# Set attention into a top-1 mixture of experts: every expert on every token, or tokens sorted on chip by expert

## The chip, the cores and the metric

The program runs on one NeuronCore of a Trainium2 chip. The metric is the device time of one execution in microseconds (us). The kernel before takes 8194.92 us, the median of three runs (8193.73 to 8201.59).

The engines are named as in the profile: PE is TensorE (PEld is its weight load), DVE is VectorE, ACT is ScalarE, POOL is GpSimd, SP is SyncE. Each works through its own list of instructions in order and waits on semaphores for the others.

## What is computed

The reference, shortened. Two steps, with B = 4 batches of N = 11456 tokens of C = 128 channels, 45824 tokens in all.

```python
def mab(q, kv):                                  # in the reference's _attn_ref
    s = scale * (q @ kv.transpose(0, 2, 1))
    s = s - s.max(-1, keepdims=True)
    a = np.exp(s); a /= a.sum(-1, keepdims=True) + 1e-09
    return a @ kv
h = mab(I, x)                                    # 32 inducing points attend to all tokens of the batch
x = mab(x, h)                                    # every token attends to the 32 rows of h

logits = x @ w_gate + modality_bias[modality_id] # 8 experts
e_idx = np.argmax(logits, axis=1)
gate_w = softmax(logits)[e_idx]
for e in range(8):                               # only the tokens whose top expert is e
    h = np.maximum(x[mask] @ w1[e], 0.0)         # 128 -> 1024
    out[mask] = gate_w[mask, None] * (h @ w2[e]) # 1024 -> 128
```

## The kernel before

All loops are unrolled; a scheduler sets the order of each engine's instructions, and the buffers of the pools (four PSUM buffers tagged pt, two for oep) set how far the engines may run ahead.

Stage one (lines 77 to 125) computes h batch by batch, 128 tokens at a time: 90 tiles of a batch, the last with 64 tokens. A tile is loaded (L90), transposed on PE in float32 (L92), copied (L94), multiplied with the inducing points (L96), and passed through a running maximum and sum (L98 to L119), in which every tile waits for the one before it.

Stage two (lines 127 to 205) takes the same 360 tiles again. Each is loaded (L135), goes through its attention (L137 to L162) and its gate (L165 to L187), and then through all eight experts: for an expert eight matmuls with 128x128 weights of w1 (L197), eight ReLUs that bring them from PSUM to SBUF as bfloat16 (L198), eight matmuls with w2 (L200), and two DVE operations that scale the result with the token's gate weight, which is zero for the seven experts that the token did not choose, and add it up (L202, L203). All DMAs go through POOL's queue: the tokens, the modality ids (L169), the weights (L65, L69) and the output (L205).

## Time and profile before

| | |
|---|---|
| median of three runs | 8194.92 us |
| the profiled execution, first to last instruction | 8197.6 us |
| PE busy | 6172.4 us, 75% |
| ACT busy | 4934.1 us, 60% |
| DVE busy | 3673.2 us, 45% |
| POOL busy | 789.4 us, 10% |
| instructions | 158845 |

The profiled execution's own time is its span; it lies 2.7 us above the median. Busy time is the time in which at least one instruction of the engine ran. Matmuls are pipelined, so that the mean duration of one is much longer than the distance from one to the next: what counts on PE is the distance. The rows come further down.

### The profile page before, as it was taken

The page shows a single profiled execution, that of the slowest core. Times are in us where ns is not written, and L with a number is a line of the kernel's source. Part 1 is how long each engine was busy: PE and PEld are TensorE (multiplying, and loading weights), DVE is VectorE, ACT ScalarE, POOL GpSimd, SP SyncE. Part 2 cuts the span into 40 slices and gives each one's busy share as a digit, 9 for nine tenths or more (in the row PEclk, how much of TensorE's full clock was granted, in tenths as well). Part 3 has the DMA queues.
Part 4 walks back from the last instruction along what each step waited for, and adds up shares of the span by engine and source line. Part 5 has one row for each costly group of instructions (what it writes and reads, how often), then busy time and mean ns, then how long its engine had stood idle before and what let it go on. Part 6 is the DMA issues. An engine that isn't in the chain of part 4 may idle for free.

```text
span 8197.6 us, 158845 instructions
## 1 busy us (share of the span) xinstructions
PE 6172.4 (75%) x51124; PEld 4334.1 (53%) x51124; DVE 3673.2 (45%) x16227; ACT 4934.1 (60%) x26281; POOL 789.4 (10%) x1452
## 2 busy tenths in 40 slices
PE   3444444488888888888888888888888888888888
PEld 1111111266666666666666666666666666666665
DVE  3444444444444444444444444444444444444444
ACT  1222222267776776767776767767766677677766
POOL 2111111100000000000000000000000000000000
PEclk9999999987888887888888878888888788888888
DMA  1000000000000000000000000000000000000000
GB/s 55 15 15 15 15 15 15 14 9 8 9 9 9 9 9 8 9 9 9 9 9 9 9 8 9 9 9 9 9 9 9 8 9 9 9 9 8 9 9 6
DMA packets 49176, 89.41 MB, mean 11 GB/s; under 512 B 29008, under 2 KB 29008, under 8 KB 48336
## 3 DMA queue, kind: packets, MB, share of 16 engines
q0 software_dynamic: 48336, 79.26, 3.4%
q8 instruction: 399, 6.54, 0.3%
q14 instruction: 441, 3.61, 0.2%
HBM read 55.71 MB, written 23.46 MB: 10 GB/s over the span
## 4 chain that ended last, share of the span: by engine, by line
PE 63%; ACT 13%; DVE 12%; issue 11%; POOL 1%; DMA 0%; ACTq 0%; POOLq 0%
PE hp L197 28%; PE oep L200 18%; ACT hid L198 6%; PE sp L96 3%; PE op L117 3%; PE xmp L160 3%; PE lp L165 2%; PE xtTp L92 2%; PE sp L141 2%; ACT pexp L108 2%; ACT ex L150 2%; PE pT L113 1%; PE aTp L156 1%; DVE xtT L94 1%; ACT alpha L105 1%
## 5 line engine op out<-in xcount | busy, mean ns | idle before, releaser
L198 ACT ACTIVATE hid<-hp 128x128 bf16<-128x128 f32 x23040 | 4305.5, 297 | 1466.8 <-PE hp L197 1277.2
L197 PE MATMUL hp<-xmb,w1sb 128*128 128x128 bf16 x23040 | 3992.6, 244 | 174.6 <-ACT hid L198 6.6
L200 PE MATMUL oep<-w2sb,hid 128*128 128x128 bf16 x23040 | 3402.3, 245 | 2.8 <-ACT hid L198 2.8
L197 PEld LDWEIGHTS <-w1sb 128*128 128x128 bf16 x23040 | 2319.1, 113 | 639.8 <-issue 403.5
L200 PEld LDWEIGHTS <-hid 128*128 128x128 bf16 x23040 | 2124.6, 106 | 658.8 <-ACT hid L198 77.5
L202 DVE TENSOR_SCALAR scaled<-oep,gm 128x128 f32<-128x128 f32 x2880 | 1010.4, 351 | 2231.8 <-PE oep L200 2231.8
L203 DVE TENSOR_TENSOR oacc<-oacc,scaled 128x128 f32<-128x128 f32 x2880 | 840.5, 292 | 98.9
L98 ACT ACTIVATE ssb<-sp 32x128 f32<-32x128 f32 x360 | 95.5, 265 | 1025.4 <-PE sp L96 1025.4
L135 POOL DMA_DIRECT2D xt<-in_x_dram x360 | 192.9, 536 | 4283.5 <-PE oep L200 4198.0
L113 PE MATMUL pT<-ident,pexp 32*128 32x32 f32 x360 | 111.3, 309 | 624.3 <-ACT pexp L108 624.3
L156 PE MATMUL aTp<-ident,a_sb 128*32 128x128 f32 x360 | 115.2, 320 | 605.7 <-DVE a_sb L154 605.7
L113 PEld LDWEIGHTS pT<-ident,pexp 32*128 32x128 f32 x360 | 63.5, 176 | 786.6 <-ACT pexp L108 786.6
L156 PEld LDWEIGHTS aTp<-ident,a_sb 128*32 128x32 f32 x360 | 34.8, 97 | 645.5 <-DVE a_sb L154 645.5
L169 POOL DMA_DIRECT2D mid<-in_moe_modality_id_dram x360 | 200.2, 556 | 1506.4 <-DVE midf L171 1451.5
L160 PE MATMUL xmp<-aT,h_sb 32*128 32x128 f32 x720 | 240.6, 427 | 133.6 <-DVE aT L158 133.6
L96 PE MATMUL sp<-xtT,indT 128*32 128x128 f32 x720 | 228.1, 420 | 141.4 <-DVE xtT L94 137.5
L90 POOL DMA_DIRECT2D xt<-in_x_dram x360 | 192.9, 536 | 1368.4 <-PE op L117 1333.3
L165 PE MATMUL lp<-wg,xm 128*128 128x8 f32 x720 | 208.9, 364 | 137.9 <-DVE xm L162 137.9
L117 PE MATMUL op<-xt,pTsb 128*32 128x128 f32 x720 | 228.5, 421 | 102.1 <-DVE pTsb L115 102.1
L165 PEld LDWEIGHTS lp<-wg,xm 128*128 128x128 f32 x720 | 175.0, 302 | 229.0 <-DVE xm L162 229.0
L143 ACT ACTIVATE ssb<-sp 128x32 f32<-128x32 f32 x360 | 70.9, 197 | 326.5 <-PE sp L141 326.5
L100 DVE TENSOR_REDUCE mnew<-ssb 32x1 f32<-32x128 f32 x360 | 98.4, 273 | 367.1 <-ACT ssb L98 367.1
(69 smaller groups left out, 3767.2 us busy)
## 6 DMA issues: line engine op xcount, KB each, us to landing
xt<-in_x_dram POOLq DMA_DIRECT2D x712, 64.0 KB, 2.1
out_dram<-oacc POOLq DMA_DIRECT2D x356, 64.0 KB, 1.8
mid<-in_moe_modality_id_dram POOLq DMA_DIRECT2D x356, 1.0 KB, 2.0
w1f<-in_moe_w_dram POOLq DMA_DIRECT2D x1, 4096.0 KB, 15.8
w2f<-in_moe_w_dram POOLq DMA_DIRECT2D x1, 4096.0 KB, 29.3
xt<-in_x_dram POOLq DMA_DIRECT2D x8, 32.0 KB, 2.0
out_dram<-oacc POOLq DMA_DIRECT2D x4, 32.0 KB, 1.8
mid<-in_moe_modality_id_dram POOLq DMA_DIRECT2D x4, 0.5 KB, 1.8
```

What stands on the lines that cost most here:

```text
L96: nc.tensor.matmul(sp[:, :r], indT, xtT[:, :r], start=True, stop=True)
L113: nc.tensor.transpose(pT[:r], pexp[:, :r], ident[:m, :m])
L117: nc.tensor.matmul(op, pTsb[:r], xt[:r], start=True, stop=True)
L156: nc.tensor.transpose(aTp[:, :r], a_sb[:r], ident[:r, :r])
L160: nc.tensor.matmul(xmp[:, :r], hb, aT[:, :r], start=True, stop=True)
L165: nc.tensor.matmul(lp[:r], xm[:, :r], wg, start=True, stop=True)
L169: nc.gpsimd.dma_start(out=mid32[:r], in_=mid_all[b * N + r0: b * N + r0 + r, :])
L197: nc.tensor.matmul(hp[:, :r], w1sb[:, e, f * 128:(f + 1) * 128], xmb[:, :r], start=True, stop=True)
L198: nc.scalar.activation(hid[:, f, :r], hp[:, :r], AF.Relu)
L200: nc.tensor.matmul(oep[:r, :], hid[:, f, :r], w2sb[:, e, f, :], start=(f == 0), stop=(f == nF - 1))
L202: nc.vector.tensor_scalar_mul(scaled[:r], oep[:r], gm[:r, e:e + 1])
L203: nc.vector.tensor_add(oacc[:r], oacc[:r], scaled[:r])
```

## The change

The stages are rebuilt batch by batch as three phases, which the program writes in the order A(0), B(0), A(1), B(1), C(0), A(2), B(2), C(1), A(3), B(3), C(2), C(3).

- Phase A (h) takes 16 tiles at once, a chunk; a batch has five chunks of 16 tiles and one of 10. One DMA on SP's queue loads 1 MB. Sixteen transposes on PE go through four DVE copies of 512 columns; four score matmuls of 512 columns and 32 rows follow, each in its own 32 columns of the array (tile_position), then one maximum, one exponential, four transposes, one copy and sixteen small matmuls with the tokens. Each chunk keeps its own maximum; the chunks are put together at the batch's end.
- Phase B computes h@W1 for all experts once (32 rows by 1024 columns for each), goes through the chunks a second time (the transposed tokens of phase A are still in SBUF), finds logits, top expert and gate weight for the whole batch, and computes for every token a slot such that the tokens of one expert stand together, padded to tiles of 256. A row of 72 bytes per token (32 attention weights as bfloat16, already multiplied with the gate weight, and the token's number) is written to that slot in DRAM: 90 indirect DMAs from POOL, 128 rows each. One DMA on SP brings the sorted list back.
- Phase C goes through the 52 sorted tiles. PE and DVE each read the tile's expert number into a register. DVE copies that expert's part of h@W1 to stg; eight matmuls with K = 32 and 256 columns give the hidden layer, four ReLUs of 512 columns (two on ACT, two on DVE) bring it to SBUF, sixteen matmuls with w2 at a register address give 256 rows of output, ACT copies them, and two indirect DMAs from POOL write the rows to their tokens.
- The weights are loaded by ACT's queue; w2 goes through the two buffers tagged xn, which the tokens use too, and is cast on POOL.

The core of the diff (`phase_b`'s gate arithmetic on whole-batch tiles and the end of phase A are cut):

```diff
...
+P = 128
+T = 256
+CH = 16
+OOB = 1 << 20
...
+    NT = (N + E * (T - 1)) // T
+    NS = NT * T // P
...
-    sb = ctx.enter_context(tc.tile_pool(name="sb", bufs=4))
-    ps = ctx.enter_context(tc.tile_pool(name="ps", bufs=4, space=bass.MemoryType.PSUM))
-    ps_big = ctx.enter_context(tc.tile_pool(name="ps_big", bufs=2, space=bass.MemoryType.PSUM))
+    xpool = ctx.enter_context(tc.tile_pool(name="xpool", bufs=2))
+    xtpool = ctx.enter_context(tc.tile_pool(name="xtpool", bufs=NCH))
+    sb = ctx.enter_context(tc.tile_pool(name="sb", bufs=2))
+    sm = ctx.enter_context(tc.tile_pool(name="sm", bufs=2))
+    bat = ctx.enter_context(tc.tile_pool(name="bat", bufs=1))
+    bat2 = ctx.enter_context(tc.tile_pool(name="bat2", bufs=2))
+    hidp = ctx.enter_context(tc.tile_pool(name="hidp", bufs=2))
+    ps_h = ctx.enter_context(tc.tile_pool(name="ps_h", bufs=2, space=bass.MemoryType.PSUM))
+    ps_o = ctx.enter_context(tc.tile_pool(name="ps_o", bufs=1, space=bass.MemoryType.PSUM))
+    ps = ctx.enter_context(tc.tile_pool(name="ps", bufs=3, space=bass.MemoryType.PSUM))
...
-    w1sb = singles.tile([D, E, F], BF)
...
+    fill = bat2.tile([P, NS, RW], I32, tag="srt")
+    nc.gpsimd.memset(fill, 0)
+    nc.gpsimd.memset(fill[:, :, m // 2:m // 2 + 1], OOB)
...
-            xt = sb.tile([P, D], F32)
-            nc.gpsimd.dma_start(out=xt[:r], in_=x[b, r0:r0 + r, :])
-            xtTp = ps.tile([D, P], F32, tag="pt")
-            nc.tensor.transpose(xtTp[:, :r], xt[:r], ident[:r, :r])
-            xtT = sb.tile([D, P], F32)
...
+        nc.scalar.dma_start(out=d.rearrange("(p s) w -> p s w", p=P), in_=fill)
...
+    def load_weights():
+        nc.scalar.dma_start(out=w1f, in_=moe_w1.rearrange("e d f -> d e f"))
+        for e in range(E):
+            w2f = xpool.tile([P, nF, D], F32, tag="xn")
+            nc.scalar.dma_start(out=w2f, in_=moe_w2[e].rearrange("(o p) d -> p o d", p=P))
+            nc.gpsimd.tensor_copy(w2sb[:, e], w2f)
...
+            nc.tensor.matmul(s[32 * g:32 * g + 32, 0:k, :], lhsT, xT.rearrange("d (i g) n -> d i g n", g=G)[:, 0:k, g, :],
+                             start=True, stop=True, tile_position=(0, 32 * g))
...
+            xn = xpool.tile([P, CH, D + 4], F32, tag="xn")
+            nc.sync.dma_start(out=xn[:, 0:nj, 0:D], in_=x[b, 0:J * P, :].rearrange("(p j) d -> p j d", j=J)[:, c * CH:c * CH + nj, :])
...
+            nc.gpsimd.memset(xn[:, :, D:D + 1], 1.0)
...
+                    nc.tensor.transpose(tp[:, k, 0:w], xn[0:w, G * i + k, 0:D], ident[:w, :w])
...
+                nc.vector.tensor_copy(xT[:, G * i:G * i + full, :], tp[:, 0:full, :])
...
+            s = scores(indT, xT, c)
...
+            nc.vector.reduce_max(mxall[:, c:c + 1], s[:, 0:nb, :], axis=AX.XY)
...
+            nc.scalar.activation(p[:, 0:nb, :], s[:, 0:nb, :], AF.Exp, bias=nbias, scale=scale)
...
+                nc.tensor.transpose(pTp[:, i, :], p[:, i, :], ident)
...
+            nc.scalar.copy(pT[:, 0:nb * G, :].rearrange("p c m -> p (c m)"), pTp[:, 0:nb, :].rearrange("p i c -> p (i c)"))
...
+                    nc.tensor.matmul(o[32 * g:32 * g + 32, :], pT[0:w, k, :], xn[0:w, k, 0:D + 1],
+                                     start=(i == mine[0]), stop=(i == mine[-1]), tile_position=(0, 32 * g))
...
+                    nc.tensor.matmul(hp[32 * g:32 * g + 32, e, :], hT, w1f[:, 2 * e2 + e, (F // G) * g:(F // G) * (g + 1)],
+                                     start=True, stop=True, tile_position=(0, 32 * g))
+            nc.scalar.copy(hw[:, 2 * e2:2 * e2 + 2, :], hp)
...
+            s = scores(hT, xTs[c], c)
...
+            nc.scalar.activation(s2[:, 0:nb, :], s[:, 0:nb, :], AF.Copy, scale=scale)
...
+                nc.tensor.transpose(tt[:, i, :], s2[:, i, :], ident)
...
+            nc.vector.reduce_max(mx[:, 0:nt], ttv, axis=AX.X)
...
+            nc.vector.tensor_tensor(exc, ttv, mx[:, 0:nt].unsqueeze(2).to_broadcast([P, nt, m]), op=OP.subtract)
+            nc.scalar.activation(exc, exc, AF.Exp)
...
+                nc.tensor.transpose(et[:, i, :], exc[:, G * i:G * i + G, :].rearrange("p g m -> p (g m)"), ident)
...
+            nc.vector.tensor_copy(eT[:, 0:full, :], et[:, 0:full, :])
...
+                nc.tensor.matmul(up[:, i, :], eT[:, i, :], bd.rearrange("p g e -> p (g e)"), start=True, stop=True)
...
+        pay = bat.tile([P, NJ, RW], I32, tag="pay")
+        nc.vector.tensor_tensor(pay.bitcast(BF)[:, :, 0:m], ex, gs.unsqueeze(2).to_broadcast([P, NJ, m]), op=OP.mult)
+        nc.gpsimd.memset(pay[:, :, m // 2 + 1:RW], 0)
+        nc.vector.tensor_scalar(pay[:, :, m // 2], tok, b * N, None, op0=OP.add)
...
+        nc.vector.tensor_tensor_scan(cum.rearrange("p e j -> p (e j)"), ones[:, 0:1].to_broadcast([P, E * NJ]), oh.rearrange("p e j -> p (e j)"), 0.0, op0=OP.mult, op1=OP.add)
...
+        row = bat2.tile([P, NJ], I32, tag="row")
+        nc.vector.scalar_tensor_tensor(row, pi[:, 0, :], float(NS), pi[:, 1, :], op0=OP.mult, op1=OP.add)
...
+        nc.vector.tensor_scalar(eidi, eid, float(E - 1), None, op0=OP.min)
...
+        for j in range(NJ):
+            w = width(j)
+            i = nc.gpsimd.indirect_dma_start(
+                out=srt_d[b][:, :], out_offset=bass.IndirectOffsetOnAxis(ap=row[0:w, j:j + 1], axis=0),
+                in_=pay[0:w, j, :], in_offset=None)
...
+        srt = bat2.tile([P, NS, RW], I32, tag="srt")
+        nc.sync.dma_start(out=srt, in_=srt_d[b].rearrange("(p s) w -> p s w", p=P))
...
+        for t in range(NT):
+            if t % 2 == 0:
+                k = min(4, NS - 2 * t)
+                etp = ps.tile([P, 4, P], BF, tag="ps")
+                rep = sb.tile([P, 4, G, m], BF, tag="rep")
+                nc.vector.tensor_copy(rep[:, 0:k], srt.bitcast(BF)[:, 2 * t:2 * t + k, 0:m].unsqueeze(2).to_broadcast([P, k, G, m]))
+                for q in range(k):
+                    nc.tensor.transpose(etp[:, q, :], rep[:, q].rearrange("p g m -> p (g m)"), identb)
+                eT4 = sb.tile([P, 4, P], BF, tag="eT4")
+                nc.vector.tensor_copy(eT4[:, 0:k, :], etp[:, 0:k, :])
+            eT = eT4[:, (t % 2) * 2:(t % 2) * 2 + 2, :]
+            ev = nc.values_load(eidi[0:1, t:t + 1], engines=(PE, DVE), min_val=0, max_val=E - 1,
+                                skip_runtime_bounds_check_because="clamped on the chip")
+            stg = sb.tile([P, 2, P], BF, tag="stg")
+            nc.vector.tensor_copy(stg, hw[:, ds(ev, 1), :].rearrange("p o (r f) -> p (o r) f", r=2))
+            hp = [ps_h.tile([P, 2, T], F32, tag=f"hp{q}", bufs=1, name=f"hp{q}") for q in range(4)]
+            for r in range(2):
+                for g in range(G):
+                    nc.tensor.matmul(hp[g][:, r, :], stg[32 * g:32 * g + 32, r, :], eT[32 * g:32 * g + 32, :, :],
+                                     start=True, stop=True, tile_position=(32 * g, 0))
+            hid = hidp.tile([P, G, 2, T], BF, tag="hid")
+            for g in range(G):
+                if g % 2 == 0:
+                    nc.scalar.activation(hid[:, g], hp[g], AF.Relu)
+                else:
+                    nc.vector.tensor_scalar_max(hid[:, g], hp[g], 0.0)
+            op = ps_o.tile([P, 2, D], F32, tag="op")
+            for s in range(2):
+                for f in range(nF):
+                    nc.tensor.matmul(op[:, s, :], hid[:, f // 2, f % 2, s * P:(s + 1) * P], w2sb[:, ds(ev, 1), f, :].rearrange("p o d -> p (o d)"),
+                                     start=(f == 0), stop=(f == nF - 1))
+            ob = sb.tile([P, 2, D], F32, tag="ob", bufs=3)
+            nc.scalar.copy(ob, op)
+            for s in range(2):
+                i = nc.gpsimd.indirect_dma_start(
...
+                    in_=ob[:, s, :], in_offset=None, bounds_check=B * N - 1, oob_is_err=False)
...
-            xmb = sb.tile([D, P], BF)
...
-            for e in range(E):
-                for f in range(nF):
-                    hp = ps.tile([P, P], F32, tag="pt")
-                    nc.tensor.matmul(hp[:, :r], w1sb[:, e, f * 128:(f + 1) * 128], xmb[:, :r], start=True, stop=True)
-                    nc.scalar.activation(hid[:, f, :r], hp[:, :r], AF.Relu)
-                for f in range(nF):
-                    nc.tensor.matmul(oep[:r, :], hid[:, f, :r], w2sb[:, e, f, :], start=(f == 0), stop=(f == nF - 1))
-                scaled = sb.tile([P, D], F32)
-                nc.vector.tensor_scalar_mul(scaled[:r], oep[:r], gm[:r, e:e + 1])
-                nc.vector.tensor_add(oacc[:r], oacc[:r], scaled[:r])
...
+    load_weights()
+    phase_a(0)
+    phase_b(0)
+    for b in range(B):
+        if b + 1 < B:
+            phase_a(b + 1)
+            phase_b(b + 1)
+        phase_c(b)
```

How the instructions stand now, at the three places on which the prediction's terms rest.

PE at the start, the first tiles of stage one before (xt is the token tile, pexp its exponentials):

```order
L92 MATMUL xtTp<-ident,xt 128x128
L96 MATMUL sp<-xtT,indT 32x128
L113 MATMUL pT<-ident,pexp 128x32
L117 MATMUL op<-xt,pTsb 32x128
L92 MATMUL xtTp<-ident,xt 128x128
```

And now, the end of chunk 0 and chunk 1 of A(0) (xn holds 16 token tiles):

```order
L214 MATMUL o_t<-xn,pT 32x129 x16
L190 MATMUL tp<-ident,xn 128x128 x16
L155 MATMUL s<-xT,indT 32x512 x4
L204 MATMUL pTp<-ident,p 128x128 x4
L214 MATMUL o_t<-xn,pT 32x129 x16
```

The same four steps stand in the same order; one round now serves 16 tiles, and nothing of the next chunk stands between the steps of one.

PE in the experts, before (the first tile of stage two):

```order
L160 MATMUL xmp<-aT,h_sb 128x128
L165 MATMUL lp<-wg,xm 128x8
L197 LDWEIGHTS w1sb
L197 MATMUL hp<-xmb,w1sb 128x128
L197 LDWEIGHTS w1sb
```

And now, between two tiles of C(0) (eidi holds the tiles' expert numbers, L427 is the matmul with w2, L416 that of the hidden layer):

```order
L427 LDWEIGHTS hid
L427 ISA
L427 MATMUL op<-w2sb,hid 128x128
L409 TENSOR_LOAD eidi
L416 LDWEIGHTS stg
L416 MATMUL hp_1959<-eT_1900,stg 128x256
```

Every matmul with w2 has an ISA instruction before it that works out its address from the register; TENSOR_LOAD fills the register once per tile; the hidden matmuls of a later tile stand among the w2 matmuls of an earlier one.

POOL before, from the end of stage one into stage two:

```order
L90 DMA xt<-in_x_dram 128x128 x89
L90 DMA xt<-in_x_dram 64x128
L135 DMA xt<-in_x_dram 128x128 x5
L169 DMA mid_15413<-in_moe_modality_id_dram 128x2
L135 DMA xt<-in_x_dram 128x128
```

And now, from the end of B(0) into C(0) (L382 is the scatter of the sorted rows, L432 that of the output):

```order
L382 DMA srt_136<-pay,row 13312x18 x90
L181 MEMSET xn 128x16 x2
L327 MEMSET pay 128x90
L181 MEMSET xn 128x16 x4
L254 MEMSET bd 128x36
L336 AFFINE_SELECT oh<-oh 128x8
L342 MEMSET prev 128x1
L432 DMA out_dram<-ob,srt 45824x128 x2
L382 DMA srt_138<-pay,row 13312x18 x90
L432 DMA out_dram<-ob,srt 45824x128 x6
```

A(1)'s memsets for its chunks 2 and 3 now stand behind the 90 scatters of batch 0, and all but two of C(0)'s output scatters behind the 90 of batch 1.

## Rows read from the trace of the kernel before

**Rows 1.** The page's line of PE's, ACT's and the other engines' busy time.

```profile
PE 6172.4 (75%) x51124; PEld 4334.1 (53%) x51124; DVE 3673.2 (45%) x16227; ACT 4934.1 (60%) x26281; POOL 789.4 (10%) x1452
```

**Rows 2.** Stretches: length, busy time by engine (count), PEclk, DMA share, GB/s.

```profile
0.00:40.00 40.00, 0.44 (x1) 0.18 (x1) 10.06 (x13) 1.28 (x1) 19.53 (x20) 1.00 0.74 217
40.00:1622.00 1582.00, 715.06 (x2164) 260.44 (x2164) 670.70 (x3633) 339.42 (x1440) 197.15 (x369) 1.00 0.05 15
1622.00:8194.00 6572.00, 5456.95 (x48959) 4073.53 (x48959) 2992.42 (x12584) 4593.38 (x24840) 572.75 (x1064) 0.81 0.03 9
```

**Rows 3.** The page's chain of work that ended last, by engine and line.

```profile
PE 63%; ACT 13%; DVE 12%; issue 11%; POOL 1%; DMA 0%; ACTq 0%; POOLq 0%
PE hp L197 28%; PE oep L200 18%; ACT hid L198 6%; PE sp L96 3%; PE op L117 3%; PE xmp L160 3%; PE lp L165 2%; PE xtTp L92 2%; PE sp L141 2%; ACT pexp L108 2%; ACT ex L150 2%; PE pT L113 1%; PE aTp L156 1%; DVE xtT L94 1%; ACT alpha L105 1%
```

**Rows 4.** Timeline in stage two: start, us, engine, line, operation, tiles.

```profile
3000.35 0.35 DVE L202 TENSOR_SCALAR scaled<-oep,gm 128x128 f32<-128x128 f32 x1 [0.89 <-PE oep L200]
...
3000.97 0.43 PEld L200 LDWEIGHTS <-hid 128*128 128x128 bf16 x5
3001.02 0.52 PE L200 MATMUL oep<-w2sb,hid 128*128 128x128 bf16 x5
...
3001.92 0.35 DVE L202 TENSOR_SCALAR scaled<-oep,gm 128x128 f32<-128x128 f32 x1 [0.89 <-PE oep L200]
```

**Rows 5.** Groups by line and shape: busy us, mean ns | idle before.

```profile
L198 ACT ACTIVATE hid<-hp 128x128 bf16<-128x128 f32 x22784 | 4263.1, 298 | 1424.9 <-PE hp L197 1238.2
...
L94 DVE COPY xtT<-xtTp 128x128 f32<-128x128 f32 x356 | 103.8, 291 | 46.9 <-PE xtTp L92 0.6
...
L137 PE MATMUL xtTp<-ident,xt 128*128 128x128 f32 x356 | 100.2, 281 | 0.0
...
L189 DVE CAST xmb<-xm 128x128 bf16<-128x128 f32 x356 | 80.6, 226 | 12.0
...
L150 ACT ACTIVATION_READ_ACCUMULATOR ex<-ssb,nmx 128x1 f32 x356 | 66.3, 186 | 0.0
...
L198 ACT ACTIVATE hid<-hp 128x64 bf16<-128x64 f32 x256 | 42.4, 226 | 41.9 <-PE hp L197 38.9 <-PE oep L200 2.7
...
L94 DVE COPY xtT<-xtTp 128x64 f32<-128x64 f32 x4 | 0.9, 225 | 0.1
```

**Rows 6.** Timeline in stage one, two tiles in succession.

```profile
44.68 0.28 DVE L118 TENSOR_TENSOR O<-O,op 32x128 f32<-32x128 f32 x1 [0.61 <-PE op L117]
...
45.43 0.64 PE L96 MATMUL sp<-xtT,indT 128*32 128x128 f32 x2 [0.38 <-DVE xtT L94]
...
49.07 0.28 DVE L118 TENSOR_TENSOR O<-O,op 32x128 f32<-32x128 f32 x1 [0.73 <-PE op L117]
```

**Rows 7.** Groups of POOL: building the descriptors of one DMA.

```profile
L169 POOL DMA_DIRECT2D mid<-in_moe_modality_id_dram x360 | 200.2, 556 | 1506.4 <-DVE midf L171 1451.5 <-DVE oacc L203 34.8 <-DMA mid<-in_moe_modality_id_dram 10.2
...
L69 POOL DMA_DIRECT2D w2f<-in_moe_w_dram x1 | 2.8, 2761 | 0.0
L51 POOL DMA_DIRECT2D indT<-in_inducing_dram x1 | 1.8, 1840 | 0.4 <-issue 0.4
```

**Rows 8.** Timeline at the start: a DVE cast and a POOL DMA beside it.

```profile
20.91 4.43 DVE L67 CAST w1sb<-w1f 128x8192 bf16<-128x8192 f32 x1 [10.05 <-DMA w1f<-in_moe_w_dram]
21.16 4.29 POOL L169 DMA_DIRECT2D mid<-in_moe_modality_id_dram  x1 [9.20 <-DMA w1f<-in_moe_w_dram]
```

**Rows 9.** DMA issues: count, KB each, median us from issue to landing.

```profile
mid<-in_moe_modality_id_dram POOLq DMA_DIRECT2D x356, 1.0 KB, 2.0
w1f<-in_moe_w_dram POOLq DMA_DIRECT2D x1, 4096.0 KB, 15.8
w2f<-in_moe_w_dram POOLq DMA_DIRECT2D x1, 4096.0 KB, 29.3
```

More of the change, by code (lines that the diff above doesn't have):

```diff
@@ new lines @@
+    identb = singles.tile([P, P], BF)
+    nc.vector.tensor_copy(identb, ident)
+    ones = singles.tile([P, P], F32)
+    nc.vector.memset(ones, 1.0)
+    tri = singles.tile([P, P], F32)
+    nc.gpsimd.affine_select(out=tri, in_=ones, compare_op=OP.is_gt, fill=0.0, base=0,
+                            pattern=[[1, P]], channel_multiplier=-1)
+    selm = singles.tile([P, m], F32)
+    nc.vector.reduce_sum(selm, ident.rearrange("p (g m) -> p m g", g=G), axis=AX.X)
+    sel = singles.tile([P, G, m], F32)
@@ new lines @@
+    for g in range(G):
+        nc.vector.tensor_copy(sel[:, g, :], selm)
+    one1 = singles.tile([1, 1], F32)
+    nc.vector.memset(one1, 1.0)
+    indT = singles.tile([D, m], F32)
+    ind_sb = sm.tile([m, D], F32, tag="ind_sb")
+    nc.sync.dma_start(out=ind_sb, in_=inducing)
+    indTp = ps.tile([D, m], F32, tag="ps")
+    nc.tensor.transpose(indTp, ind_sb, ident[:m, :m])
+    nc.vector.tensor_copy(indT, indTp)
+    wg = singles.tile([D, E], F32)
+    nc.sync.dma_start(out=wg, in_=moe_w_gate)
@@ new lines, in chunk_tiles, with blocks, width, scores @@
+    def chunk_tiles(c):
+        return list(range(c * CH, min((c + 1) * CH, NJ)))
+    def blocks(c):
+        t = chunk_tiles(c)
+        return (len(t) + G - 1) // G
+    def width(j):
+        return P if j < J else R
+    def scores(lhsT, xT, c):
+        nb = blocks(c)
+        s = ps.tile([P, 4, P], F32, tag="ps")
+        for g in range(G):
+            full = [i for i in range(nb) if c * CH + G * i + g < J]
+            k = len(full)
+            nc.tensor.matmul(s[32 * g:32 * g + 32, 0:k, :], lhsT, xT.rearrange("d (i g) n -> d i g n", g=G)[:, 0:k, g, :],
+                             start=True, stop=True, tile_position=(0, 32 * g))
+            for i in range(k, nb):
+                j = c * CH + G * i + g
+                w = width(j) if j < NJ else 0
+                lo = 0
+                if w:
+                    nc.tensor.matmul(s[32 * g:32 * g + 32, i, 0:w], lhsT, xT[:, G * i + g, 0:w], start=True, stop=True, tile_position=(0, 32 * g))
+                nc.tensor.matmul(s[32 * g:32 * g + 32, i, w:P], lhsT, xT[:, g, w:P], start=True, stop=True, tile_position=(0, 32 * g))
+        return s
@@ new lines, with phase_c @@
+    out2 = out
+    def phase_c(b):
+        st = state[b]
+        hw, srt, eidi = st["hw"], st["srt"], st["eidi"]
+        eT4 = None
+        for t in range(NT):
[15 more added lines that the diff above has]
+            for r in range(2):
+                for g in range(G):
+                    nc.tensor.matmul(hp[g][:, r, :], stg[32 * g:32 * g + 32, r, :], eT[32 * g:32 * g + 32, :, :],
+                                     start=True, stop=True, tile_position=(32 * g, 0))
+            hid = hidp.tile([P, G, 2, T], BF, tag="hid")
+            for g in range(G):
+                if g % 2 == 0:
[11 more added lines that the diff above has]
+                i = nc.gpsimd.indirect_dma_start(
+                    out=out2[:, :], out_offset=bass.IndirectOffsetOnAxis(ap=srt[:, 2 * t + s, m // 2:m // 2 + 1], axis=0),
+                    in_=ob[:, s, :], in_offset=None, bounds_check=B * N - 1, oob_is_err=False)
+                tc.declare_no_dep(i.ins, group="out", reason="tokens are unique")
+                tc.add_to_no_dep_group("out", i.ins)
```

342 lines of the change are left out of this document (216 added, 126 removed).

## The prediction, made before the changed kernel was timed

> **What bounds the kernel now.** I read four views in this order. The busy line [rows 1] shows no engine above 75%, so an average tells little, and the stretches [rows 2] split the span: 40 us of start, 1582 us of stage one, 6572 us of stage two, 80% of the 8197.6 us. Stage two has 360 tiles, so 18.3 us each. The chain [rows 3] puts PE first, with the expert matmuls L197 and L200 alone at 46% of the span. The timeline [rows 4] shows the beat: from the scaling of one expert to that of the next are 3001.92 - 3000.35 = 1.57 us, in which PE does 16 matmuls, 98 ns each; five in a row without a wait load weights in 0.43 us, 86 ns each. So stage two is 360 x 8 experts x 1.57 us = 4520 us of experts, and the remaining 2050 us, 5.7 us a tile, is the chain of small steps between two tiles. Stage one is a chain too: 4.39 us from one tile's L118 to the next [rows 6], 360 times, while its PE is busy 45% of the stretch [rows 2].
>
> **What the change takes away.** Seven of eight experts: 360 x 128 = 46080 expert matmuls become 4 x 52 tiles x (8 + 16) = 4992. And the chains: 16 tiles go through one round instead of one. The forecast is therefore not a difference but a new sum, built from durations in these rows. It has three unknown prices that no row shows: m, the time of a sorted tile of 256 tokens in phase C; d, POOL's time for one indirect DMA; and AB, the time of phases A and B of a batch.
>
> **m.** PE: 16 matmuls with w2 at 98 ns [rows 4], 1.57 us. Each has an ISA instruction that works out an address: below, nothing (it hides under the weight load before it); above, 186 ns, the shortest row of an instruction that only moves engine state (the accumulator read) [rows 5], 3.0 us in all. I take 0.1 us, half of that row, since it too goes through the sequencer one by one: 1.6 us. Eight hidden matmuls of 256 columns in four row groups: 8 x 0.17 (twice the 86 ns) = 1.4 us one after another, a quarter of it if the four run at once; I take 0.8. Two transposes 0.2. One TENSOR_LOAD: between nothing, since it stands several rows before its use, and 2.0 us, the landing of a 1 KB DMA [rows 9]; I take 0.4, because PE is one stream but the array still holds work. Sum 4.6, and I use m = 4.5. Beside it ACT has two ReLUs of 512 columns, by the slope of the L198 rows [rows 5] 0.298 + 384 x 0.072/64 = 0.73 us, and one copy of 256, 0.44: 1.9 us. DVE has two of 512 at 0.291 + 384 x 0.066/64 = 0.69 us, a staging copy of 256 (0.3 from the 226 ns cast), and every second tile one repeat and one PSUM copy (0.5 + 0.69): 2.3 us. Both lie beside PE. The ends for m are 2.5 (DVE, with a hand-over of the single op buffer) and 1.57 + 3.0 + 1.4 + 0.2 + 2.0 = 8.1.
>
> **d.** A plain DMA of 128 rows costs POOL 0.56 us; one of 4096 single elements 1.84 us, one of 8192 pieces 2.76 us [rows 7]. An indirect one has 128 rows but must read an index for each, so it lies between: I take 1.2, bounds 0.54 and 2.76. Landing is 2.0 us [rows 9], but eight may be under way, so the landing doesn't limit it. S = 90 d = 108 us is the scatter of a batch.
>
> **AB.** Phase A, a chunk of 16 tiles: 16 transposes at 0.2 us (between the 86 ns beat and 281 ns alone [rows 5]), then the last copy of 0.69: 4.0 us. Four score matmuls of 512 columns in float32: a pair for 128 columns takes 0.64 us [rows 6]; with two thirds of it, 0.43, growing with the columns (an estimate: the rest is the way through the array), 512 take 1.7 us; 6.8 one after another, 1.7 at once; I take 3.0, nearer the lower end because each holds its own 32 columns of the array. Maximum and bias 1.0, exponential 0.8, four transposes 0.9, ACT's copy 0.7, sixteen small matmuls 4.0 (0.43 each if serial, and four in a row share one column group). That is 14.4 us, 5.6 chunks: 81 us. Phase B's chunk, by the same prices: scores 3.0, copy 0.7, transposes 0.9, maximum and subtraction 1.4, exponential 0.7, transposes 0.9, copy 0.7, the last matmuls 1.2, waits 0.4: 9.9 us, 55 us in all. The end of A (a dozen tiny steps) 9, h@W1 10, the gate of the whole batch 18 (13 operations of 720 columns at 0.8 us, one of 2880, twenty small ones at 0.15). AB = 173 us; all prices at their ends give 130 and 215.
>
> The Trainium skill, page "TensorE: Matmul & The Clock Gate", section "Part 3: Packing small matmuls — row/col tiling", says that matmuls in different column groups run at once and gives 2.38 times for three. By it the four score matmuls would take an estimated 2.9 us. No row here shows it, since the kernel before has no such matmul; if they ran one after another the sum would rise by (6.8 - 3.0) x 5.6 x 2 x 4 = 170 us.
>
> **How the parts lie in time.** POOL's order decides (the third listing in the change). The scatter of batch 0 starts when B(0) ends, and A(1) can go on for about two and a half chunks (35 us): then its small matmuls need the memset that stands behind the 90 scatters. So S is paid nearly in full there. At the end of B(1) the same: all but two of C(0)'s output DMAs are queued behind S; with three ob buffers, four tiles fit in before PE must wait. So C is S + 48 m. A(2) starts on PE after C(0), and so on.
> Start: w1 is 4 MB in 15.8 us [rows 9], ACT waits for it before the fills of the sorted lists (4 x 0.96 MB, at w1's rate 14 us), then eight w2 loads go two by two through the buffers that the first token chunks need: 55 us until phase A can start (ends 45 and 75), against 40 before.
> Sum: 55 + AB 173 + S 108 + (AB - 35) 138 + three times (S 108 + 48 x 4.5 = 216 and, twice, AB 173) + 52 x 4.5 = 234 + 5. That is 55 + 173 + 108 + 138 + 324 + 648 + 346 + 234 + 5 = 2031 us. In short T = 717 + 360 d + 196 m. The profiled span and the median of the runs before differ by 0.03%, so nothing is added for that.
>
> One row speaks against putting 776 DMAs on POOL: while DVE's cast of w1 ran 4.43 us, a 128-row DMA beside it took POOL 4.29 us instead of 0.56 [rows 8]. If DVE's two SBUF copies of a tile (about 0.55 us) hold POOL up that way, a tile costs POOL 2.4 + 0.55 = 2.95 us, still under m, and nothing is added; where POOL is the bound (below) 196 x 0.55 = 108 us are.
> The Trainium skill, page "SBUF — State Buffer", section "Who interferes with whom", states the rule: a DVE operation in a two-port mode and GpSimd exclude each other for the whole instruction. The trace agrees, with those 4.29 us.
>
> **The rivals.**
> 1. Register work bounds phase C. For it: nothing in the trace shows an address from a register, and it stands 16 times in each tile. Against it: the weight load before it gives it 86 ns of cover. At the upper end, m = 8.1: 717 + 432 + 1588 = 2737 us; from m = 6 on I count it here (2325).
> 2. POOL bounds. At d = 2.76 two output DMAs are 5.5 us, more than m: 717 + 994 + 196 x 5.5 = 2789 us, with DVE in the way 2900. Against it: 128 rows are far fewer pieces than 8192.
> 3. Everything runs as smoothly as plain work: m = 2.5, d = 0.54: 717 + 194 + 490 = 1401 us. For it: the scheduler mixes two tiles on PE, so waits are filled. Against it: it needs all three prices at the low end.
> 4. Slower than before: POOL builds an indirect DMA row by row, each row a small job of its own. All 776 stand in one queue, so T = 717 + 776 d, and it passes 8195 at d = 9.6 us, 75 ns a row. The dearest POOL row is 2.76 us [rows 7], a third of that.
> 5. The sort gains less than its count: 52 tiles for 44.75 of tokens is built in, 16% of phase C, and inside the sum already; there is no way back to eight experts.
>
> **How the numbers follow.** Forecast 2031 us (m from 3.2 to 6, d from 0.8 to 2: 1630 to 2610), chance 0.47. Rival 1 0.20, rival 2 0.12, rival 3 0.18, rival 4 0.02, others 0.01. The range runs from 1500, which takes in the upper half of rival 3, to 2700, which takes in most of rival 1 and leaves out most of rival 2. A difference of 0.2%, 16 us, is about what a measurement of this kernel can tell from none; only rival 4 ends on the other side. Faster 0.97, same 0.01, slower 0.02.
>
> **What would show it.** In phase C: the distance between two ob copies, 4.5 us, with PE the bound; ISA or issue time between w2 matmuls would be rival 1, ob copies waiting for POOL's DMAs rival 2. The scatter L382: 90 DMAs in 108 us, three gaps of about 90 us in which PE and ACT stand still before C, and one in A(1). First token transposes at 55 us. A chunk of A every 14 us, of B every 10. Wrong would be a phase C in which DVE or ACT is the bound, scatters that hide under other work, or a first chunk at 40 us or before.

## The result, and the profile after

The changed kernel takes **1900.42 us** (1898.82 to 1900.96, four runs) against 8197.38 us before (8193.73 to 8201.59): a ratio of **0.2318, 95% interval 0.2314 to 0.2321**, 4.3 times faster. The forecast was 2031 us in a range of 1500 to 2700. Measured again beside the experiments the same kernel took 1988 us (`c1_after`; 1987 us in `c2_after`), with the difference in the stretches around the scatters and 2% in phase C, so each experiment is compared with the one of the two that its own trace resembles: e1 to e4, e4b, e6 and e14 with 1988, and e7, e9 and e12 with 1900.

The page of the changed kernel, with the busy line that answers to [rows 1], three of its slice lines, and the groups that matter:

```profile
PE 1160.1 (61%) x7765; PEld 662.5 (35%) x7765; DVE 613.3 (32%) x1347; ACT 393.1 (21%) x745; POOL 785.5 (41%) x841
...
PE   0666410564303999766510699966550089999998
...
POOL 2000277100777555100277655500047755555555
PEclk9875555755555555775555555576555555555555
...
L427 PE MATMUL op<-w2sb,hid 128*128 x3328 | 483.9, 290 | 320.1 <-ACT ob L430 309.8
L432 POOL DMA_INDIRECT out_dram<-ob,srt x416 | 409.2, 984 | 372.0 <-ACT ob L430 292.9
...
L423 DVE TENSOR_SCALAR hid<-hp 128x512 bf16<-128x512 f32 x416 | 278.0, 689 | 525.9 <-ACT ob L430 183.8
L382 POOL DMA_INDIRECT srt<-pay,row x360 | 348.1, 967 | 118.7 <-issue 108.5
...
L421 ACT ACTIVATE hid<-hp 128x512 bf16<-128x512 f32 x416 | 245.3, 597 | 304.0 <-PE hp L416 236.0
L430 ACT COPY ob<-op 128x256 f32<-128x256 f32 x208 | 77.4, 372 | 526.1 <-DMA out_dram<-ob,srt 318.1
L214 PE MATMUL o_t<-xn,pT 128*32 128x129 f32 x720 | 95.1, 403 | 107.8 <-POOL xn L181 89.7
```

PE's 51124 matmuls [rows 1] are now 7765, of which 3328 with w2 and 1664 with the hidden weights. PE's slices show four dips, and POOL's line has its 7s exactly there: the four scatters. The clock line is mostly 5s, the 1.2 GHz level, where the kernel before had 0.81 on average in stage two [rows 2].

The stretches of the changed kernel (start, A(0), B(0), the second part of batch 0's scatter, the rest of A(1) with B(1), batch 1's scatter, C(0)). Columns: stretch, length, busy us and instructions of each engine, granted clock, DMA share, GB/s:

```profile
0.00:52.00 52.00, 0.28 (x1) 0.18 (x1) 4.51 (x27) 0.00 (x0) 12.48 (x32) 1.00 0.83 270
52.00:134.00 82.00, 54.15 (x365) 37.97 (x365) 24.99 (x53) 9.01 (x14) 0.77 (x6) 0.81 0.28 81
134.00:224.00 90.00, 45.59 (x250) 26.81 (x249) 39.51 (x77) 10.93 (x18) 3.19 (x3) 0.57 0.00 0
...
252.00:336.00 84.00, 0.00 (x0) 0.00 (x0) 0.00 (x0) 0.00 (x0) 63.88 (x67) 0.50 0.05 7
340.00:476.00 136.00, 78.97 (x491) 49.21 (x490) 54.78 (x116) 16.79 (x29) 5.97 (x10) 0.60 0.12 36
476.00:590.00 114.00, 17.21 (x128) 9.05 (x127) 10.99 (x29) 6.83 (x13) 86.49 (x90) 0.50 0.06 8
600.00:771.00 171.00, 169.66 (x1167) 90.87 (x1166) 77.31 (x173) 69.13 (x135) 91.28 (x93) 0.51 0.10 33
```

And three of the longest waits (engine, tile and line, what released it; us in total, times, the longest):

```profile
ACT ob L430 <- DMA out_dram<-ob,srt: 318.1, 3, 106.2
PE op L427 <- ACT ob L430: 309.8, 6, 103.1
...
DVE pay L328 <- DMA srt<-pay,row: 287.0, 3, 97.2
```

Between 252 and 336 us PE, DVE and ACT do nothing at all while POOL issues 67 scatter DMAs. The ob copy waits three times for about 106 us, behind the scatters of batches 1, 2 and 3, and in C(0) PE is busy for 169.66 of 171 us, at a clock of 0.51.

### The profile page after: what moved, and what is told of

It is laid out like the page before. It is cut to its first block, busy times and chain, and to the rows that moved or that the text cites. A ratio compares the mean times of both kernels' runs of the same rounds, so it can differ in the third digit from the quotient of the medians.

```text
span 1897.1 us, 24060 instructions
## 1 busy us (share of the span) xinstructions
PE 1160.1 (61%) x7765; PEld 662.5 (35%) x7765; DVE 613.3 (32%) x1347; ACT 393.1 (21%) x745; POOL 785.5 (41%) x841
## 5 line engine op out<-in xcount | busy, mean ns | idle before, releaser
L427 PE MATMUL op<-w2sb,hid 128*128 x3328 | 483.9, 290 | 320.1 <-ACT ob L430 309.8
L432 POOL DMA_INDIRECT out_dram<-ob,srt x416 | 409.2, 984 | 372.0 <-ACT ob L430 292.9
L427 PEld LDWEIGHTS <-hid 128*128 128x128 bf16 x3328 | 313.2, 122 | 509.4 <-issue 396.8
L423 DVE TENSOR_SCALAR hid<-hp 128x512 bf16<-128x512 f32 x416 | 278.0, 689 | 525.9 <-ACT ob L430 183.8
L382 POOL DMA_INDIRECT srt<-pay,row x360 | 348.1, 967 | 118.7 <-issue 108.5
L416 PE MATMUL hp<-eT,stg 32*128 32x256 bf16 x1664 | 319.3, 393 | 4.1 <-DVE stg L412 2.4
L421 ACT ACTIVATE hid<-hp 128x512 bf16<-128x512 f32 x416 | 245.3, 597 | 304.0 <-PE hp L416 236.0
L430 ACT COPY ob<-op 128x256 f32<-128x256 f32 x208 | 77.4, 372 | 526.1 <-DMA out_dram<-ob,srt 318.1
L214 PE MATMUL o_t<-xn,pT 128*32 128x129 f32 x720 | 95.1, 403 | 107.8 <-POOL xn L181 89.7
L416 PEld LDWEIGHTS <-stg 32*128 32x128 bf16 x1664 | 72.5, 101 | 130.3 <-issue 123.1
```

The costliest lines, as they stand in the source:

```text
L214: nc.tensor.matmul(o[32 * g:32 * g + 32, :], pT[0:w, k, :], xn[0:w, k, 0:D + 1], start=(i == mine[0]), stop=(i == mine[-1]), tile_position ...
L382: i = nc.gpsimd.indirect_dma_start(out=srt_d[b][:, :], out_offset=bass.IndirectOffsetOnAxis(ap=row[0:w, j:j + 1], axis=0), in_=pay[0:w, j, ...
L416: nc.tensor.matmul(hp[g][:, r, :], stg[32 * g:32 * g + 32, r, :], eT[32 * g:32 * g + 32, :, :], start=True, stop=True, tile_position=(32 * ...
L421: nc.scalar.activation(hid[:, g], hp[g], AF.Relu)
L423: nc.vector.tensor_scalar_max(hid[:, g], hp[g], 0.0)
L427: nc.tensor.matmul(op[:, s, :], hid[:, f // 2, f % 2, s * P:(s + 1) * P], w2sb[:, ds(ev, 1), f, :].rearrange("p o d -> p (o d)"), start=(f ...
```

## The experiments

The questions: what is in the 3.7 us of a tile in phase C (theory H: an array at 1.2 GHz; theory Q: PE's instruction stream with its register steps, the prediction's rival 1), what the price of a scatter is made of, and whether the queue order alone makes the engines stand still beside it. Only e4b, e6 and e14 have the changed kernel measured on their own chip; the others are compared with a measurement from another one, and a difference of one or two per cent is not read from them. "A tile" below is the mean distance of the last 45 ob copies of a batch, averaged over the batches: 3.78 us in the changed kernel, 3.86 us in `c1_after`.

**e1: a constant address for w2.**

```diff
-  hid[...], w2sb[:, ds(ev, 1), f, :].rearrange("p o d -> p (o d)"),
+  hid[...], w2sb[:, 0, f, :],
```

> The 16 matmuls with w2 of a tile read a constant address (expert 0 for every tile, so the second layer is the wrong expert's); the register step in front of each (FUSED_REGOPS in the trace, 55 ns) falls away, everything else stays. In the changed kernel's trace a tile of phase C takes 3.70 us. Theory H (the array at 1.2 GHz sets the beat, the register step hides under it): still 3.6 to 3.7 us a tile, 1880 to 1905 us in all. Theory Q (PE's instruction stream sets the beat, the register step stands in series in it): 16 x 0.055 = 0.88 us less, 2.8 us a tile, 1900 - 196 x 0.88 = 1728 us. Theory Q2 (as Q, and with a denser stream the granted clock rises to 2.4 GHz, so that POOL's two output DMAs of 1.28 us become the bound): 2.6 us a tile, 1900 - 196 x 1.1 = 1684 us or less.

Measured: 1931 us, 57 less than 1988; a tile takes 3.61 us instead of 3.86. So sixteen register steps cost at most 0.25 us, 0.016 each: a small part of the 55 ns that one lasts in the trace, and far less than the 0.1 of the forecast. A part of it is the clock, as the stretch from 650 to 800 us shows, first in `c1_after` and then in e1 (length, busy us, granted clock, DMA share, GB/s):

```profile
650.00:800.00 150.00, 147.57 (x998) 77.74 (x996) 68.36 (x154) 58.81 (x116) 76.45 (x78) 0.50 0.10 33
```

```profile
650.00:800.00 150.00, 142.74 (x1067) 79.81 (x1067) 71.76 (x161) 62.19 (x123) 81.69 (x83) 0.57 0.10 33
```

Counted only over groups of four tiles whose granted clock was 0.50 in both, a tile takes 3.65 us instead of 3.85, so 0.20 us belong to the steps at that clock. First the row of the changed kernel (view of line 427 from 600 to 740 us: duration min/median/max in ns), then PE's timeline in e1, which shows what fills the tile instead:

```profile
L427 PEldq FUSED_REGOPS  x606: 51/55/55, 600.1 to 739.6; - x152
```

```profile
701.24 0.39 PE L416 MATMUL hp<-eT,stg 32*128 32x256 bf16 x1
701.57 0.39 PE L427 MATMUL op<-w2sb,hid 128*128 128x128 bf16 x2
701.89 0.39 PE L416 MATMUL hp<-eT,stg 32*128 32x256 bf16 x1
...
702.87 1.25 PE L427 MATMUL op<-w2sb,hid 128*128 128x128 bf16 x10
704.04 0.60 PE L416 MATMUL hp<-eT,stg 32*128 32x256 bf16 x4
```

Ten w2 matmuls in a row take 704.04 - 702.87 = 1.17 us up to the next hidden one, 0.117 each. One hidden matmul alone holds the next w2 matmul back by 0.33 us (701.24 to 701.57), while four hidden ones together last 0.60. The order mixes two tiles on PE, so the row groups seldom run four at a time. At the 1.2 GHz level the register steps are nearly hidden: theory H is the nearer one, though 57 us is more than it allowed. What the rest is, e3 and e7 show.

**e2: half the rows of each scatter.**

```diff
-  w = width(j)
+  w = min(width(j), P // 2)
```

> Each scatter DMA into the sorted list carries 64 rows instead of 128 (the other half of the tokens is left out of the sort); the number of DMAs stays at 90 a batch. Measured before: 1.27 us from one to the next. If the price is per DMA: still 1.27 us, 1895 to 1905 us in all. If it is per row: 0.64 us, 360 x 0.63 = 229 us less, about 1670 us. A fixed part f and a part per row lie between: T = 1900 - 360 x (1.27 - d).

Measured: from one scatter to the next 1.200 us instead of 1.272. So 64 rows cost 0.07 us, 1.1 ns a row, and 1.13 us are the price of a DMA whatever it carries. In all 2001 us, 13 more than 1988, though the scatters together are 25 us shorter; the wait behind a scatter did not end earlier, and why is open.

**e3: the hidden matmuls all in one row group.**

```diff
-  stg[32*g:32*g+32, r, :], eT[32*g:32*g+32, :, :], ..., tile_position=(32*g, 0)
+  stg[0:32, r, :], eT[0:32, :, :], ..., tile_position=(0, 0)
```

> The eight hidden matmuls of a tile all use row group 0 (so all compute the first 128 hidden channels of each half, with the wrong result), instead of four row groups; same number, same columns. If the four row groups run at once in the changed kernel and the array is the bound, then eight matmuls of 256 columns, 0.213 us each at 1.2 GHz, now run one after another: 1.7 us instead of about 0.43 to 0.6, 1.1 to 1.3 us more a tile, 1900 + 196 x 1.2 = 2135 us. If they were serial already: 1900 us. If PE's instruction stream is the bound and the array has slack, only a part shows: 1950 to 2080 us.

Measured: 2075 us, 87 more than 1988; a tile takes 4.28 us instead of 3.86 (208 x 0.42 = 87). So the row groups do run beside each other, but this is worth a third of the 1.2 us that four at a time would give. It was the "part only" case. The mixing seen in e1 is the likelier reason than slack in the array, since PE was busy for all of the stretch from 650 to 830 us, but no run separates the two.

**e4 and e4b: nothing of A(1) behind the scatters in POOL's queue.**

```diff
-  nc.gpsimd.memset(xn[:, :, D:D + 1], 1.0)
+  nc.vector.memset(xn[:, :, D:D + 1], 1.0)
-  nc.sync.dma_start(out=srt, in_=srt_d[b]...)
+  nc.gpsimd.dma_start(out=srt, in_=srt_d[b]...)
```

> The memset of the ones column of a token chunk goes from POOL to DVE, and the reload of the sorted list from SP's queue to POOL's, so nothing of A(1) stands behind the 90 scatters of batch 0. Theory (queue order alone makes the stall): the 90 us wait in A(1) goes, the scatter of batch 0 hides under A(1) and the chunks of B(1), the other three stay: 76 to 88 us less, about 1820 us. Rival 1 (another thing holds A(1): the token loads or the sorted list's buffers): 1880 to 1900 us. Rival 2 (DVE's copies and POOL's DMA work hold each other up while they overlap, as in the kernel before, where a POOL DMA took 4.29 us beside a DVE cast): the scatter or A(1) becomes longer, 1840 to 1880 us.

> The changed kernel once more, as the comparison on this chip for the two runs beside it and for the four earlier runs. There, three kernels with phases A and B unchanged began the scatter of batch 1 at 494 us instead of 476 us, and DVE and ACT stood still, with nothing named in the trace that released them, while POOL issued the scatter. If that comes with the edits: 1895 to 1905 us, batch 1's scatter at 476 us. If it comes with the chip or the run: 1960 to 2000 us, batch 1's scatter at 494 us.

> The ones column's memset on DVE and the reload of the sorted list on POOL's queue, as before (there 1986 us, and the wait in A(1) stayed at 66 + 20 us though POOL's queue no longer stood in its way). Theory 1 (queue order makes the stall): 76 to 88 us less than the changed kernel beside it. Theory 2 (while POOL issues scatters back to back, the other engines' releases come late, whatever the queue order): within 10 us of the changed kernel beside it, with PE and DVE still nearly idle in the stretch of batch 0's scatter.

Measured: 1986 us (e4) and 1984 us (e4b); the changed kernel on e4b's chip took 1988. Taking the wait away gave nothing there. The stretch of batch 0's scatter in `c1_after`, and PE's timeline in it:

```profile
252.00:336.00 84.00, 3.66 (x12) 1.97 (x11) 0.98 (x2) 0.00 (x0) 63.99 (x66) 0.50 0.10 20
```

```profile
256.28 0.37 PE L190 MATMUL tp<-ident,xn 128*128 128x128 f32 x1 [1.73 <-issue]
257.70 0.37 PE L190 MATMUL tp<-ident,xn 128*128 128x128 f32 x1 [1.04 <-issue]
322.45 1.11 PE L190 MATMUL tp<-ident,xn 128*128 128x128 f32 x4 [64.38 <-issue]
```

Here PE had not come to the POOL memset at all: its transposes crawl, one in 1.4 to 2.1 us, and then stand for 64 us, with no wait that the profile can name ("issue"), until the scatter is nearly done. The time is that of theory 2 in e4b's expectation, for this set of runs; that the releases come late is its guess, and no run shows it. In the run of the changed kernel that gave 1900 us the same stretch began with PE at full pace and stopped at the memset; e9 and e12 show what it does then without it.

**e6: A(b+1), C(b), B(b+1).** The edit of e4, the memset of phase B's small matrix on DVE, and:

```diff
         if b + 1 < B:
             phase_a(b + 1)
-            phase_b(b + 1)
         phase_c(b)
+        if b + 1 < B:
+            phase_b(b + 1)
```

> As the run before it, and the program's order is A(b+1), C(b), B(b+1) instead of A(b+1), B(b+1), C(b), and the memset of phase B's small matrix goes to DVE too, so that each scatter lies beside A of the next batch, which needs nothing from POOL. Theory 1 (queue order): from 224 us on, three times A 82 + rest of the scatter 37 + C 192 + B 90, then the last scatter 119 and C 192: 224 + 1203 + 311 = 1738 us, 160 us less than the changed kernel. Theory 2 (the other engines starve while POOL issues scatters): A(b+1) makes the progress of some 25 us beside each scatter and the rest of it comes after: 1860 to 1930 us, no gain.

Measured: 1955 us, 33 less than 1988, where queue order alone promised 160; PE worked 3.46 us of the 84 beside batch 0's scatter. Theory 2 again, in size somewhat better than its "no gain".

**e9: three forms of scatter, in the order of e6.** Batch 1 without the declaration that the scatters don't depend on each other; batch 2 with `bounds_check=0, oob_is_err=False`.

> The order of the run with A(b+1), C(b), B(b+1), so that A of the next batch lies beside the scatter, in three forms: batch 0 as it was; batch 1 with each scatter DMA waiting for the one before to land; batch 2 with a bound on the index so that the rows are skipped and no data is written (the tokens of batch 2 get no output); what is looked at is PE's progress through A beside each. Seen so far: beside batch 0's scatter PE did 25 us of work in 113 us. If the rate of issue is what holds the other engines up: batch 1's scatter lasts 90 x (1.0 + 2.1 to 2.4) = 280 to 310 us and A(2) beside it runs its 82 us undisturbed; batch 2 as batch 0. If the data written to DRAM is what holds them up: batch 2's A(3) runs undisturbed, 82 us, batch 1 is slow. If it is POOL's making of descriptors, whatever the rate: all three are slow. In time: rate 1955 + 185 = 2140 us; data 2140 - 75 = 2065 us.

Measured: 1892 us, in a single execution. None of the three forms held the other engines up. The stretches: batch 0's (as in the fence above, now 24.09 us of PE work instead of 3.66), batch 1's first 84 us, batch 2's,

```profile
252.00:336.00 84.00, 24.09 (x180) 16.12 (x176) 10.59 (x27) 3.61 (x6) 63.89 (x67) 0.62 0.21 52
631.00:715.00 84.00, 47.30 (x340) 33.11 (x338) 21.66 (x53) 7.04 (x12) 24.60 (x25) 0.70 0.27 73
1162.00:1277.00 115.00, 44.09 (x324) 30.54 (x322) 17.87 (x42) 6.74 (x11) 87.85 (x90) 0.65 0.14 34
```

and, from the waits beside batch 0's scatter:

```profile
DVE pay L328 <- DMA srt<-pay,row: 52.0, 1, 52.0
```

In all three A's chunks run at their usual pace (batch 0: the small matmuls of the chunks start at 224.63, 236.92, 248.83, 261.07, 272.85, 283.82). Here neither data nor rate nor descriptors stopped the engines, and since the standstill did not come at all, this run can't tell which of them, if any, makes it in the other set. Two prices come out. With all but one row out of bounds the scatters are 1.288 us apart, so the price is POOL's own work on the DMA and not the writing; when each waits for the last, 2.40 in the median and 2.67 on average. The wait in the last line was hidden by the other one before (in the changed kernel DVE waited 92.7 us for `pay` while PE waited 89.7 us for the memset): DVE's next step for A(1) stands behind the write to `pay` for batch 1, which waits for the scatter to have read it.

**e7: hidden matmuls on the whole array.** The staged weights of a tile go into a block-diagonal tile, zero elsewhere, by four copies of 32 partitions; three small tiles keep one buffer to make room.

```diff
-  nc.vector.tensor_copy(stg, hw[:, ds(ev, 1), :]...)
+  stg = stgz[t % 2]
+  for g in range(G):
+      nc.vector.tensor_copy(stg[32*g:32*g+32, g], hw[32*g:32*g+32, ds(ev, 1), :]...)
...
-  nc.tensor.matmul(hp[g][:, r, :], stg[32*g:32*g+32, r, :], eT[32*g:32*g+32, :, :], ..., tile_position=(32*g, 0))
+  nc.tensor.matmul(hp[g][:, r, :], stg[:, g, r, :], eT, start=True, stop=True)
```

> The eight hidden matmuls of a tile use the whole array: the staged weights lie in a block-diagonal tile whose other blocks are zero, so each matmul takes all 128 rows of the four-fold attention tile and no row groups are mixed with full-array matmuls; same columns (8 x 256), one after another; three more DVE copies a tile. In the run with a constant w2 address, a w2 matmul behind a hidden one started 0.32 us after it instead of 0.107 us, and the clock stayed at 1.2 GHz in phase C with PE over 95% busy. Theory R (mixing row groups and full array costs drains, and this work never lifts the clock): hidden matmuls on all rows lift the clock to 2.4 GHz in most of phase C, 8 x 0.107 + 16 x 0.06 and the register steps: 2.6 to 3.0 us a tile with POOL (2 x 1.28) near the bound, 160 to 250 us less than the changed kernel on the same chip (1988 on the last one: 1740 to 1830 us). Theory H (half clock whatever the form): 8 x 0.213 + 16 x 0.107 + transposes 0.2 = 3.6 us and register steps 0.27: 3.8 to 3.9 us, within 20 us of the changed kernel.

Measured: 1806.5 us, 94 less than 1900; a tile takes 3.31 us instead of 3.78. C(0) from 600 to 740 us, first in the changed kernel, then in e7 with two of its groups there (columns of the groups: busy us, mean ns, idle before):

```profile
600.00:740.00 140.00, 138.76 (x963) 73.92 (x963) 63.05 (x143) 56.81 (x111) 75.57 (x77) 0.51 0.12 38
```

```profile
600.00:740.00 140.00, 130.56 (x1080) 95.58 (x1078) 113.89 (x288) 61.62 (x126) 83.93 (x86) 0.99 0.12 38
...
L430 PE MATMUL op<-w2sb,hid 128*128 x677 | 98.7, 217 | 9.4 <-issue 4.3 <-ACT hid L424 2.2 <-DVE stgz L416 1.2
...
L420 PE MATMUL hp<-eT,stgz 128*128 128x256 bf16 x332 | 54.0, 273 | 0.0
```

The granted clock is 0.99, the 2.4 GHz level, against 0.51 at the 1.2 GHz level, with PE no busier than before. A w2 matmul lasts 217 ns instead of 290 on average, a hidden one 273 instead of 393 (its mean in the changed kernel). The changes between row groups and whole array went too: from 600 to 770 us in the changed kernel a w2 matmul starts 0.35 us after the hidden one before it and a hidden one 0.23 us after the w2 matmul before it (medians), 0.58 us for the two; in e7 these are 0.11 and 0.055. At half the clock e7's 0.165 would be an estimated 0.33 and not 0.58, so the mixing counts beside the clock; what each is worth in time this run doesn't separate. Whether the row groups would do as well with the hidden matmuls of several tiles in one go, unmixed, was not tried. Theory R, at half its size: expected were 2.6 to 3.0 us a tile. DVE, with the three extra copies, is busy for 81%, and the register steps are still there; e14 shows what they cost at this clock.

**e12: e7 and e6 together.**

> The hidden matmuls on the whole array together with the order A(b+1), C(b), B(b+1) and the memsets and the reload moved as in the two runs before. If the two add up: as the run with the whole array alone, less the 33 us that the order gave on the last chip (160 us where the other engines don't stand still beside the scatter): theory R 1710 to 1800 us, theory H 1950 us. Rival: with phase C shorter than 2.6 us a tile POOL is the bound and its queue also carries the reload: 20 to 40 us more than that sum.

Measured: **1684 us** (1680.5 to 1685.3), 0.2055 of the kernel before (0.2051 to 0.2058), 216 us less than the changed kernel's 1900 and 122 less than e7. The scatter of batch 0 and C(0):

```profile
252.00:336.00 84.00, 20.03 (x150) 13.48 (x146) 7.77 (x22) 3.60 (x6) 63.07 (x66) 0.59 0.19 44
350.00:517.00 167.00, 155.61 (x1315) 115.29 (x1314) 137.43 (x350) 73.79 (x152) 99.25 (x101) 1.00 0.12 37
```

PE goes through A(1) beside the scatter, so in this set of runs what stood behind the scatters in the queues was the cause of the stall. The order gave 122 of the 160 us; the wait for `pay` seen in e9 keeps the end of A behind the scatter.

**e14: e12, with w2 staged by ACT and two payload buffers.** To make room the sorted list and the h@W1 tile have one buffer each.

```diff
+  w2t = hidp.tile([P, nF, D], BF, tag="w2t")
+  nc.scalar.copy(w2t..., w2sb[:, ds(ev, 1), :, :]...)      # and w2t[:, f, :] in the matmul
-  pay = bat.tile([P, NJ, RW], I32, tag="pay")
+  pay = bat2.tile([P, NJ, RW], I32, tag="pay")
```

> The run with the whole array and the new order, with two things more. First, ACT copies the tile's w2 (1024 columns) into a staged tile, so PE's matmuls have constant addresses and no register step; seen there: 3.31 us a tile at 2.4 GHz, w2 matmuls 0.133 us apart, the distance of the register steps. Theory Q (at 2.4 GHz PE's instruction stream is the bound): PE falls to about 8 x 0.107 + 16 x 0.056 + 0.15 = 1.9 us and DVE (2.75 us busy a tile there) becomes the bound: 2.8 to 2.9 us a tile, 94 us less. Rival: ACT, with 1.57 + 0.9 us, or the hand-over of the single output bank sets the beat: 3.2 us, no gain. Second, two buffers for the payload, since in the trace DVE stood 52 us before the end of A(1) in a write to the payload that the scatter still read: the end of A and h@W1 go under the scatter, 3 x 9 to 14 us less. Together 1684 - 94 - 35 = 1555 us (theory Q), or 1640 us (rival).

> The changed kernel as it is, beside the run before on the same chip: 1895 to 1905 us if this chip is as the first, 1980 to 1990 us if it is as the second.

Measured: 1869 us, beside a changed kernel of 1987; in this set PE again crawled beside the scatter (6.73 of 84 us), so the payload's second buffer can't be judged. Phase C can: 3.46 us a tile, where e7 and e12 have 3.31 and 3.32. About half of that difference is the 2% by which phase C differs between the two sets; but of the 2.8 to 2.9 of theory Q nothing came. The rival: ACT's copy of w2 costs at least what the steps it removes cost.

```profile
412.00:582.00 170.00, 122.67 (x1352) 91.40 (x1352) 125.98 (x347) 116.27 (x201) 99.38 (x101) 0.95 0.11 36
...
L424 ACT ACTIVATE hid<-hp 128x512 bf16<-128x512 f32 x100 | 56.3, 603 | 6.2 <-PE etp L408 3.2 <-PE hp L420 1.7 <-remote 1.2
L428 ACT COPY w2t<-w2sb 128x1024 bf16 x49 | 51.4, 1048 | 0.0
```

PE is down to 72% busy, but ACT carries 1.05 us more a tile and stands at 68%, DVE at 74%; no engine is full, and the tile reads as a chain of hand-overs between the three.

Theory Q was right about PE all the same. PE's timeline in e7, with the steps, and in e14, without, both at a granted clock of 1.00:

```profile
665.28 1.47 PE L430 MATMUL op<-w2sb,hid 128*128 x10 [0.25 <-DVE stgz L416]
666.59 0.60 PE L420 MATMUL hp<-eT,stgz 128*128 128x256 bf16 x4
```

```profile
480.93 0.85 PE L432 MATMUL op<-w2t,hid 128*128 128x128 bf16 x12
481.62 0.60 PE L420 MATMUL hp<-eT,stgz 128*128 128x256 bf16 x4
```

Ten w2 matmuls in e7 take 666.59 - 665.28 = 1.31 us, twelve in e14 481.62 - 480.93 = 0.69; over C(0) the median distance is 133 ns with a register step and 56 without. So the steps that are nearly hidden at 1.2 GHz cost some 77 ns each at 2.4 GHz, 1.2 of e7's 3.31 us a tile.

## Why the forecast held, step by step

**The formula.** T = 717 + 360 d + 196 m with the measured d = 1.272 us and m = 3.71 us (the 47 distances in C(0) from the ob copy at 596.68 us to that at 771.22) gives 717 + 458 + 727 = 1902 us, 2 us from the result. So the structure, start, AB and which stretches lie one after another, was right, though 2 us is closer than its parts deserve (see AB), and the miss of 131 us is d, +26, and m, -155.

**m, the mis-sized term.** Of the 4.5 us, the register steps were taken at 1.6 and cost 0.20 to 0.25 (e1). The sixteen w2 matmuls were taken at 98 ns, 1.57 us; at 1.2 GHz they take 0.117 each up to the next hidden one (e1), 1.87. The eight hidden matmuls were taken at 0.8; what is left for them with the two transposes is 3.7 - 0.25 - 1.87 = 1.6 us, since they come one or two at a time between w2 matmuls. The TENSOR_LOAD taken at 0.4 leaves no gap that the busy time shows, PE being busy for 169.66 of 171 us. So two terms were too dear and two too cheap; that they partly cancel is luck. And one condition was in no term: the 98 ns come from a stretch of the kernel before [rows 4] in which the granted clock was 1.00,

```profile
3000.00:3004.00 4.00, 3.74 (x42) 2.58 (x41) 1.77 (x6) 3.71 (x22) 0.00 (x0) 1.00 0.00 0
```

and phase C ran at 0.51. At that clock the register steps were nearly hidden (e1). That PE is the bound, and neither DVE, ACT nor POOL, held.

**d.** 1.2 forecast, 0.967 busy and 0.30 of issue measured; S is 113.3 us for 108. The ends of the range were never near: rival 2 (2.76) and rival 4 fall, the latter with 1.1 ns a row against the 75 it needed (e2). The row that spoke against POOL [rows 8] did not come back: beside DVE's copies the 416 output DMAs took 0.98 to 1.04 us each.

**AB.** 172 us for 173, with errors that cancel, which is luck: A with its end took 82 us (52 to 134) instead of 90, at 12 us a chunk instead of 14, and B 90 (134 to 224) instead of 83, with its chunks at the forecast 10. The four score matmuls of a chunk, taken at 3.0 us, run at once: the records of one pass start within 0.02 us of each other. From PE's timeline of the changed kernel, at a granted clock of 1.00 (each matmul leaves two records):

```profile
233.94 1.06 PE L155 MATMUL s<-xT,indT 128*32 128x512 f32 x8 [1.14 <-DVE xT L192]
```

The estimate from the Trainium skill, page "TensorE: Matmul & The Clock Gate", section "Part 3: Packing small matmuls — row/col tiling", was 2.9 us; the trace shows more concurrency than that page's figure for three column groups. What was taken too small is the gate of the whole batch at the end of B: 27 us, from 197 to 224, instead of 18, with more large DVE steps than were counted (0.9 us for 720 columns, 3.17 for 2880) and copies of A(1) between them.

**The parts in time.** Start 52 us (55 forecast). The stall in A(1), and the three before C of about 106 us (forecast: about 90), came at the forecast places, and the four tiles that fit in before them too (from 472 to 485 us).

**The rivals.** Rival 1 is wrong in cause and size at 1.2 GHz (e1), but at 2.4 GHz register work does set the pace of the w2 matmuls (e7, e14). Rival 3's low prices came for the register steps, not for the rest. Nothing of rival 5 showed.
